# Other starting steps for the background work of a three-layer kernel on one TensorE

## The chip, the cores and the metric

The kernel runs on one core of a Trainium2 chip. The metric is the device time of one execution in microseconds (us); less is better. Inputs and output lie in the chip's memory; the weights arrive as 64-bit floats, everything else as 32-bit floats.

## The reference, cut to what matters

```python
def _attn_ref(q, k, v):                      # q, k, v: (8, 8, 576, 64)
    q_s = exp(q - max(q, -1));  q_s /= sum(q_s, -1) + 1e-9
    k_s = exp(k - max(k, 2));   k_s /= sum(k_s, 2) + 1e-9
    return q_s @ (k_s^T @ v)                 # per batch and head
x = attn.transpose(0, 2, 1, 3).reshape(4608, 512)
h = x @ w_in                                 # (512, 2048)
x = max(0.01 * h, h) @ w_out                 # (2048, 512)     layer A
h = max(max(x @ w1, x @ w2), x @ w3)         # (512, 768) each
out = h @ w_out2                             # (768, 512)      layer B
```

## The kernel before, in words

The 4608 tokens are nine chunks of 512. Every matrix product is done in three matmuls of 32-bit halves (high by high, high by low, low by high), 128 by 128 by 512, so an operand first has to be split into a high and a low part: ScalarE (ACT) copies the high part, VectorE (DVE) subtracts it.

**Foreground.** The foreground is counted in steps. Steps 0 to 47 are layer A for chunks 0 to 2, one step for one of the 16 blocks of 128 hidden columns (24 matmuls: `project` and `a_out`). Steps 48 to 79, 80 to 111 and 112 to 143 are layer A for the chunk pairs (3, 4), (5, 6), (7, 8), by a seven-product scheme. In each pair a left half has eight rounds `t` of three steps; a round has seven products of six matmuls (`product_a`, L798, weights in tiles `group`) and four fills of six (`out_a`, L570, weights in tiles `outw`). The right half has 16 blocks `m` of 12 matmuls, two to a step, and reads a new `outw` tile of 1 MB every step. Then come layer B for chunk 0 (six blocks `m`, L1172) and, to the end, layer B for four pairs, which has no background beside it.

**Background.** `background(step)` is called once in a step, and twice from step 28 to 47. It starts the generators whose time has come (`plan_units`, `ahead_units`) and moves each running one to its next `yield`. They are: attention of later chunks (`kv_unit`, `q_unit`: two loads, reductions, exponentials, small matmuls, for each chunk and pair of heads); `sums_a`, the weight sums of layer A (eight, each two loads, four additions, a split, stores to `stream_in`); `ahead_unit` u = 0 to 8, layer B's first weights (two loads, each converted from 64 bits by `split_words`; sums; two splits; stores to `stream` and `plainw`); `ahead_out` m = 0 to 5, layer B's second weights (one load, one conversion, one store `wo`); and `join`, which adds the partial results of chunks 0 and 1.

**What sets the order.** A planner puts the instructions on each engine in the order in which its own timeline has them ready, the earlier written first. Background work on DVE is tied to its step by a one-column copy from the newest `g` (L165, L322). The loads of `group` and `outw` are pinned: each is issued behind the last DMA written before it. All DMAs are issued by one queue, SP's, in order; an issue that waits holds up every one behind it. `group` and `outw` are loaded two tiles ahead.

**Buffers that matter.** `wp` has 17 tiles of 8 KB a partition, shared by weights, operands and rooms. `xp` has two tiles each of `xhi` and `xlo`; rooms of `ahead_unit` and `ahead_out` alternate between the two. `ca` is a single buffer: each conversion and each high part (`hi`) of an `ahead_unit` takes it in turn, and a `hi` keeps it until its stores have landed.

Of the kernel before, what the change touches and what calls it, by code (L numbers as in the profile page):

```python
# [18 lines left out]
P = 128  # L19
# [7 lines left out]
CONV = 3  # L27
HALVES = 28
APAIRS = ((3, 4), (5, 6), (7, 8))
AUSES = ("a11", "a12", "s2", "s1", "s3", "a22", "s4")  # L30
# [39 lines left out]
def tile_kernel(ctx: ExitStack, tc: tile.TileContext, q, k, v, wa, wb, out):  # L70
# [72 lines left out]
    def post():  # L143

        for f in posted[:]:
            f()
        posted.clear()

    def split_words(raw, hi, lo, n, after=None, whole=None, keep=None):

        if raw.dtype != I64:
            if whole is not None:
                nc.vector.tensor_copy(whole, raw.rearrange("p (b n) -> p b n", n=H))
                return
            if keep is not None:
                posted.append(lambda: nc.sync.dma_start(keep, raw[:, :N]))
            nc.scalar.activation(hi, raw, AF.Copy)
            nc.vector.tensor_tensor(lo, raw, hi.bitcast(F32), op=ALU.subtract)
            return
        words = raw.bitcast(U32).rearrange("p (n t) -> p n t", t=2)  # L160
        high, low = words[:, :, 1], words[:, :, 0]
        a = cp.tile([P, 2 * N], U32, tag="ca", name="ca")[:, :n]
        af, bf = a.bitcast(F32), high.bitcast(F32)
        if after is not None:
            nc.scalar.activation(af[:, 0:1], after[:, 0:1], AF.Copy)  # L165
        nc.scalar.activation(af, bf, AF.Abs)
        nc.vector.tensor_scalar(af, af, MOST_HIGH, LEAST_HIGH, op0=ALU.min, op1=ALU.max)
        nc.vector.tensor_scalar(a, a, 3, 0x3FFFFFF8, op0=ALU.logical_shift_left, op1=ALU.bitwise_and)
        nc.vector.scalar_tensor_tensor(a, high, 0xC0000000, a, op0=ALU.bitwise_and, op1=ALU.bitwise_or)
        if whole is None:  # L170
            nc.scalar.activation(hi, af, AF.Copy)
        nc.vector.tensor_scalar(high, a, 0xFF800000, None, op0=ALU.bitwise_and)
        nc.vector.scalar_tensor_tensor(bf, low, 2.0**-52, bf, op0=ALU.mult, op1=ALU.mult)
        if whole is not None:
            af, bf = (t.rearrange("p (b n) -> p b n", n=H) for t in (af, bf))
            nc.vector.tensor_tensor(whole, af, bf, op=ALU.add)
            return
        nc.vector.tensor_tensor(af, af, bf, op=ALU.add)
        nc.vector.tensor_tensor(lo, af, hi.bitcast(F32), op=ALU.subtract)
        if keep is not None:  # L180
            copy = raw.bitcast(F32)[:, :N]
            nc.scalar.activation(copy, af[:, :N], AF.Copy)
            posted.append(lambda: nc.sync.dma_start(keep, copy))

# [54 lines left out]

    def a_room():  # L240
        rooms.append(xp.tile([P, 4 * N], F32, tag=("xhi", "xlo")[len(rooms) % 2], name="room"))
        return rooms[-1]

    def ahead_unit(u):

        t, j = UNITS[u]
        room = a_room()
        b = room.rearrange("p (b n) -> p b n", n=H)
# [24 lines left out]
    def ahead_out(m):  # L273
        room = a_room()
        raw = room[:, 2 * N :].bitcast(wb.dtype)[:, :N]
# [40 lines left out]
    def behind_step(column):  # L316
# [4 lines left out]
        if "g" in newest:  # L321
            nc.scalar.activation(column, newest["g"][:, 0:1], AF.Copy)  # L322

    def hurried(c):
        return CONV <= c < CONV + 2

# [8 lines left out]
    def kv_unit(b, hp, early):  # L335
# [46 lines left out]
        else:  # L382
# [7 lines left out]
            nc.scalar.activation(ke, ke, AF.Exp)  # L390
            if hurried(b):
                yield
        yield
# [49 lines left out]
    def q_unit(c, hp, early):  # L443
# [69 lines left out]
        yield  # L513
        if hurried(c):
            yield
        while not kv_done(c, hp):
# [120 lines left out]
    def sums_a(t):  # L637

        room = wp.tile([P, 4 * N], F32, tag="w", name="room")
        b = room.rearrange("p (b n) -> p b n", n=H)  # L640
# [21 lines left out]
    def plan_units(c):  # L662

        early = c < EARLY
        for hp in range(NP):
            if c == 2:
                start, lag = 2 * hp + 13, 2
            elif c < CONV + 2:
                start, lag = HALVES + (c - CONV) * 6 + 1.5 * hp, 1
            else:  # L670
                i, at = divmod(c - CONV, 2)
                start, lag = CONV * MA + 2 * MA * (i - 1) - 8 + 3 * (4 * at + hp), 2
            if c < B:
                yield start, kv_unit(c, hp, early)
            if c == EARLY:
                yield HALVES, split_kv_unit(c - 1, hp)
            yield start + lag, q_unit(c, hp, early)
# [23 lines left out]
    def ahead_units():  # L701
        for m in range(MA):
            yield max(BEGUN[m] + 3, 8), stage_a(m)
        for t in range(MA // 2):
            yield HALVES + 2 + 2.5 * t, sums_a(t)
        for u, at in enumerate((52, 64, 84, 100, 112, 116, 124, 128, 132)):
            yield at, ahead_unit(u)
        for m, at in enumerate((90, 94, 119, 122, 135, 137)):
            yield at, ahead_out(m)
        for c, at in enumerate((112, 123)):  # L710
            yield at, join(c)
# [121 lines left out]
    for turn in turns:  # L833
# [3 lines left out]
        for m in range(*turn[1:]):  # L837
# [14 lines left out]
            if step == 0:  # L852
# [7 lines left out]
                conv_a(2, x_tiles(1)[0][:, NP - 1].bitcast(F32))  # L860
            if step >= HALVES:
                background(step + 0.5)
            step += 1
            if step > CONV * MA - 4:
                if not begun_a:
                    building = a_operands(0, begun_a)
                    begun_a["begun"] = True
                for _ in range(3 if step < CONV * MA else 99):
                    next(building, None)
            if step == CONV * MA - 2:  # L870
                for i in range(AHEAD_A + 1):
# [17 lines left out]
    def store_pair(i, side, f, acc):  # L889
# [7 lines left out]

        posted.append(rows)

# [25 lines left out]
    for i in range(len(APAIRS)):  # L925
# [47 lines left out]
        for m in range(MA - 2):  # L973
# [10 lines left out]
            if last and m == 11:  # L984
                cur = split_x2(loaded)
            if m == 2 and not last:
                building = a_operands(i + 1, nxt)
            if 2 <= m:
                for _ in range(1 if m < MA - 3 else 99):
# [5 lines left out]
        fills = [lambda f=f, i=i, pairs=pairs: out_a(i, 1, MA // 2 - 1, f, pairs) for f in range(KDM)]  # L995
    assert not live and not waiting
    att_ctx.close()
    bp.append(ctx.enter_context(tc.tile_pool(name="bp", bufs=1)))

    def store_rows(i, c, col, acc):  # L1000
# [171 lines left out]
    for m in range(MB):  # L1172
        if m < 4:
            for i in range(4 + 2 * m, 6 + 2 * m):
                load_b(i)
        accs3 = [project_b(m, j, cur) for j in range(3)]
        g = f32_tile()
# [9 lines left out]
        else:  # L1187
            b_out(*prev)
        if m == 1:
            ops = {}  # L1190
            building = operands(quarters_b(sides), ops, operand)
        if m >= 2:
            for _ in range(2 if m < MB - 1 else 99):
                next(building, None)
        if m == 3:
            for i in range(AHEAD):
                load_group(i)
        prev = (0, m, hpair)
# [92 lines left out]
```

## Time and profile before

| | |
|---|---|
| median of three runs | 1484.92 us (1484.3 to 1485.85) |
| profiled execution | 1488.23 us, its span 1486.4 us |
| TensorE busy | 1405.0 us, 95% |
| VectorE, ScalarE busy | 886.2 us (60%), 679.7 us (46%) |
| moved by DMA | 343.99 MB, 231 GB/s over the span |
| steps 24 to 47 | about 177 to 351 us |
| pair 0, left and right half | about 351 to 496 and 496 to 558 us |
| pair 1, left and right half | about 558 to 676 and 676 to 728 us |
| pair 2, left and right half | about 728 to 868 and 868 to 938 us |
| layer B of chunk 0 | about 938 to 1000 us |

The stages are cut where the count of matmuls of each line says that a step begins; the planner lets a round's first product slip before the end of the stage ahead of it, so the edges are not sharp. The granted clock (PEclk) is the share of TensorE's full 2.4 GHz in a stretch; its other level is 1.2 GHz. A busy TensorE at a low clock does less.

### The profile page before, as it was taken

The page shows a single profiled execution, that of the slowest core. Times are in us where ns is not written, and L with a number is a line of the kernel's source. Part 1 is how long each engine was busy: PE and PEld are TensorE (multiplying, and loading weights), DVE is VectorE, ACT ScalarE, POOL GpSimd, SP SyncE. Part 2 cuts the span into 40 slices and gives each one's busy share as a digit, 9 for nine tenths or more (in the row PEclk, how much of TensorE's full clock was granted, in tenths as well). Part 3 has the DMA queues.
Part 4 walks back from the last instruction along what each step waited for, and adds up shares of the span by engine and source line. Part 5 has one row for each costly group of instructions (what it writes and reads, how often), then busy time and mean ns, then how long its engine had stood idle before and what let it go on. Part 6 is the DMA issues. An engine that isn't in the chain of part 4 may idle for free.

```text
span 1486.4 us, 18291 instructions
## 1 busy us (share of the span) xinstructions
PE 1405.0 (95%) x6624; PEld 1138.1 (77%) x6624; DVE 886.2 (60%) x1468; ACT 679.7 (46%) x1400; POOL 25.3 (2%) x42
## 2 busy tenths in 40 slices
PE   7999999998999899999997766999999999999999
PEld 5788877786888678887775655888888888888887
DVE  9888958987676836748556564323562463454332
ACT  6766846665565636645343332312242233233222
POOL 0000001000000000000000000000000000000000
PEclk9999999999999999999998988999999999999999
DMA  9487957555866855777988887947334724634701
GB/s 375 163 285 250 319 194 225 159 195 178 338 245 252 286 230 217 273 285 284 372 301 314 299 294 238 408 175 282 142 114 135 286 89 184 241 142 140 280 13 57
DMA packets 127194, 343.99 MB, mean 231 GB/s; under 512 B 11392, under 2 KB 68224, under 8 KB 102656
## 3 DMA queue, kind: packets, MB, share of 16 engines
q1 hardware_dynamic: 127104, 342.83, 63.4%
q8 instruction: 52, 0.85, 0.2%
q14 instruction: 38, 0.31, 0.1%
HBM read 257.33 MB, written 85.46 MB: 231 GB/s over the span
## 4 chain that ended last, share of the span: by engine, by line
PE 79%; DMA 8%; DVE 7%; ACT 3%; issue 2%; SPq 1%; DVEq 0%; ACTq 0%
PE ps L798 36%; PE acc L570 31%; PE ps L570 10%; DMA outw<-stream_out 1%; PE ps L398 1%; DMA room<-wi 1%; PE ps L522 1%; DMA spare<-in_v_dram 1%; DMA stream<-hi 1%; DMA spare<-in_k_dram 1%; DVE opA L759 1%; DVE glo L591 1%; DMA stream_out<-w 1%; DMA raw<-in_wa_dram 1%; DMA room<-in_wb_dram 1%
## 5 line engine op out<-in xcount | busy, mean ns | idle before, releaser
L798 PE MATMUL ps<-op,group 128*128 128x512 f32 x1512 | 352.8, 389 | 0.7 <-ACT snap L1090 0.7
L798 PEld LDWEIGHTS ps<-op,group 128*128 128x128 f32 x1512 | 283.6, 188 | 60.2 <-ACT snap L1090 1.3
L570 PE MATMUL acc<-ghi,outw 128*128 128x512 f32 x768 | 255.2, 400 | 36.0 <-DMA outw<-stream_out 33.9
L798 PE MATMUL ps<-opA,group 128*128 128x512 f32 x1008 | 252.4, 396 | 11.7 <-DMA group<-stream_in 7.8
L798 PEld LDWEIGHTS ps<-opA,group 128*128 128x128 f32 x1008 | 189.2, 190 | 56.0 <-DMA group<-stream_in 8.2
L570 PEld LDWEIGHTS acc<-ghi,outw 128*128 128x128 f32 x768 | 147.2, 193 | 71.0 <-issue 35.0
L570 PE MATMUL acc<-glo,outw 128*128 128x512 f32 x384 | 154.0, 401 | 4.4 <-DVE glo L591 4.4
L570 PE MATMUL acc<-wB,h 128*128 128x512 f32 x576 | 140.4, 389 | 0.1
L570 PE MATMUL acc<-ghi,w 128*128 128x512 f32 x384 | 128.3, 397 | 3.6 <-ACT ghi L590 3.6
L570 PE MATMUL ps<-xhi,w 128*128 128x512 f32 x384 | 128.9, 401 | 1.3 <-ACT g L845 0.7
L1090 ACT ACTIVATE snap<-ps 128x512 f32<-128x512 f32 x108 | 61.8, 598 | 143.8 <-PE ps L798 143.2
L570 PEld LDWEIGHTS acc<-wB,h 128*128 128x128 f32 x576 | 108.0, 188 | 23.3 <-ACT h L1114 0.5
L1105 DVE TENSOR_TENSOR snap<-snap,ps 128x512 f32<-128x512 f32 x72 | 49.4, 686 | 119.0 <-ACT snap L1090 92.4
L591 DVE TENSOR_TENSOR glo<-g,ghi 128x512 fp32r<-128x512 f32 x102 | 69.8, 687 | 46.6 <-ACT ghi L590 46.1
L570 PEld LDWEIGHTS acc<-glo,outw 128*128 128x128 f32 x384 | 74.1, 193 | 23.1 <-DVE glo L591 7.7
L570 PEld LDWEIGHTS ps<-xhi,w 128*128 128x128 f32 x384 | 73.5, 192 | 18.3 <-ACT g L845 1.1
L570 PEld LDWEIGHTS acc<-ghi,w 128*128 128x128 f32 x384 | 72.1, 189 | 20.0 <-ACT ghi L590 4.7
L1101 DVE TENSOR_TENSOR best<-snap,ps 128x512 f32<-128x512 f32 x36 | 24.7, 687 | 93.7 <-PE ps L798 43.8
L590 ACT ACTIVATE ghi<-g 128x512 fp32r<-128x512 f32 x102 | 63.6, 628 | 29.1 <-PE acc L570 13.8
L570 PE MATMUL acc<-glo,w 128*128 128x512 f32 x192 | 75.6, 394 | 1.0 <-DVE glo L591 1.0
L570 PE MATMUL ps<-xlo,w 128*128 128x512 f32 x192 | 76.2, 398 | 0.1
L1114 ACT ACTIVATE h<-best 128x512 fp32r<-128x512 f32 x48 | 30.3, 632 | 95.6 <-DVE best L1107 95.2
(159 smaller groups left out, 1799.7 us busy)
## 6 DMA issues: line engine op xcount, KB each, us to landing
group<-stream SPq DMA_DIRECT2D x64, 1024.0 KB, 6.6
outw<-stream_out SPq DMA_DIRECT2D x48, 1024.0 KB, 8.8
group<-stream_in SPq DMA_DIRECT2D x42, 1024.0 KB, 8.9
raw<-in_wa_dram SPq DMA_DIRECT2D x16, 1024.0 KB, 7.6
room<-in_wb_dram SPq DMA_DIRECT2D x24, 512.0 KB, 5.4
x<-st SPq DMA_DIRECT2D x40, 256.0 KB, 2.9
wB<-plainw SPq DMA_DIRECT2D x9, 1024.0 KB, 14.3
stream_out<-w SPq DMA_DIRECT2D x16, 512.0 KB, 4.2
```

The costliest lines, as they stand in the source:

```text
L398: nc.tensor.matmul(acc[z, : D + 1], lhsT=ke[:, r, z], rhs=vt[:, r, h], start=r == 0, stop=r == RK - 1)
L522: nc.tensor.matmul(both(xps, c0, c1), lhsT=a, rhs=halves(y, c0, c1), start=i == 0, stop=i == 2)
L570: nc.tensor.matmul(acc, lhsT=l, rhs=r, start=first and i == 0, stop=last and i == 2)
L590: nc.scalar.activation(hi[:, z], g[:, z], AF.Copy)
L591: nc.vector.tensor_tensor(lo[:, z], g[:, z], hi[:, z].bitcast(F32), op=ALU.subtract)
L759: nc.vector.tensor_tensor(o[:, 1, z], t[:, z], o[:, 0, z].bitcast(F32), op=ALU.subtract)
L798: nc.tensor.matmul(bank, lhsT=l, rhs=r, start=fresh and first, stop=last, skip_group_check=not fresh)
L1090: nc.scalar.activation(t, bank, AF.Copy)
L1101: nc.vector.tensor_tensor(g, snap, bank, op=ALU.add)
L1105: nc.vector.tensor_tensor(snap, snap, bank, op=ALU.add)
L1114: nc.scalar.activation(h[:, m, 0], g, AF.Copy)
```

## The change

It changes no arithmetic of the result. Attention of chunks 3 and 4 starts at the steps of `HURRIED`, three to four steps earlier, and later chunks' five steps later and closer together; a yield is added in both generators. Four of the eight `sums_a` move from steps 30 to 47 into pair 0. The nine `ahead_unit`s and six `ahead_out`s get other steps: none is left in pair 0, five pieces lie in pair 1, and the last two begin in layer B's first blocks, where `background` is now called nine times more. The last three units and two outs take their rooms from `wp`. Operands of the next pair are built from block 5 of the right half, not 2; those of pair 0 over five steps. The store of the first weights' copy (`keep`) is written two background calls later. Layer B's own pool, operands and weights 8 to 11 come at its block 3.

```diff
+HURRIED = ((24, 2), (26, 2), (28, 1), (29.5, 1), (31, 1), (32.5, 1), (34, 1), (35.5, 1))
     def post():
-        for f in posted[:]:
+        now = [f for wait, f in posted if wait == 0]
+        posted[:] = [(wait - 1, f) for wait, f in posted if wait]
+        for f in now:
             f()
-        posted.clear()
...
-            posted.append(lambda: nc.sync.dma_start(keep, copy))
+            posted.append((2, lambda: nc.sync.dma_start(keep, copy)))
...
-    def a_room():
+    def a_room(wide=False):
+        if wide:
+            return wp.tile([P, 4 * N], F32, tag="w", name="room")
...
-        room = a_room()                       # ahead_unit
+        room = a_room(t == 2)
...
-        room = a_room()                       # ahead_out
+        room = a_room(m >= 4)
...
-            if hurried(b):                    # kv_unit, behind the exponential
-                yield
+            yield
...
-        if hurried(c):                        # q_unit, ahead of its matmuls
-            yield
+        yield
...
-        room = wp.tile([P, 4 * N], F32, tag="w", name="room")    # sums_a
+        room = a_room(t < 4)
...
             elif c < CONV + 2:
-                start, lag = HALVES + (c - CONV) * 6 + 1.5 * hp, 1
+                start, lag = HURRIED[4 * (c - CONV) + hp]
             else:
                 i, at = divmod(c - CONV, 2)
-                start, lag = CONV * MA + 2 * MA * (i - 1) - 8 + 3 * (4 * at + hp), 2
+                start, lag = CONV * MA + 2 * MA * (i - 1) - 3 + 2.5 * (4 * at + hp), 2
...
-                yield HALVES, split_kv_unit(c - 1, hp)
+                yield 27, split_kv_unit(c - 1, hp)
...
-            yield HALVES + 2 + 2.5 * t, sums_a(t)
-        for u, at in enumerate((52, 64, 84, 100, 112, 116, 124, 128, 132)):
+            yield (30, 34, 38, 42, 49, 53, 57, 61)[t], sums_a(t)
+        for u, at in enumerate((88, 93, 98, 112, 117, 122, 133, 137, 141)):
             yield at, ahead_unit(u)
-        for m, at in enumerate((90, 94, 119, 122, 135, 137)):
+        for m, at in enumerate((103, 107, 127, 131, 144, 147)):
             yield at, ahead_out(m)
-        for c, at in enumerate((112, 123)):
+        for c, at in enumerate((112, 124)):
             yield at, join(c)
...
-            if step >= HALVES:
-                background(step + 0.5)
-            step += 1
-            if step > CONV * MA - 4:
+            building_a = step >= CONV * MA - 5
+            if building_a:
                 if not begun_a:
                     building = a_operands(0, begun_a)
                     begun_a["begun"] = True
-                for _ in range(3 if step < CONV * MA else 99):
+                next(building, None)
+            if step >= HALVES:
+                background(step + 0.5)
+            if building_a:
+                for _ in range(1 if step < CONV * MA - 1 else 99):
                     next(building, None)
+            step += 1
...
-            if m == 2 and not last:
+            if m == 5 and not last:
                 building = a_operands(i + 1, nxt)
-            if 2 <= m:
+            if 5 <= m:
...
     load_b(3)
     for m in range(MB):
-        if m < 4:
-            for i in range(4 + 2 * m, 6 + 2 * m):
-                load_b(i)
-        accs3 = [project_b(m, j, cur) for j in range(3)]
+        for i in {0: (4, 5), 1: (6, 7), 3: (8, 9, 10, 11)}.get(m, ()):
+            load_b(i)
+        if m == 3:
+            assert not live and not waiting and not posted
+            att_ctx.close()
+            bp.append(ctx.enter_context(tc.tile_pool(name="bp", bufs=1)))
+            ops = {}
+            building = operands(quarters_b(sides), ops, operand)
+            for i in range(AHEAD):
+                load_group(i)
+        accs3 = []
+        for j in range(3):
+            accs3.append(project_b(m, j, cur))
+            if m < 3:
+                background(step)
+                step += 1
...
-        if m >= 2:
-            for _ in range(2 if m < MB - 1 else 99):
+        if m >= 3:
+            for _ in range(3 if m < MB - 1 else 99):
                 next(building, None)
```

## Rows read from the trace of the kernel before

**Rows 1.** The page's first part: busy us, share of the span, instructions.

```profile
PE 1405.0 (95%) x6624; PEld 1138.1 (77%) x6624; DVE 886.2 (60%) x1468; ACT 679.7 (46%) x1400; POOL 25.3 (2%) x42
```

**Rows 2.** Stretches by stage: length, busy (instructions) by engine, clock, DMA share, GB/s.

```profile
177.00:351.00 174.00, 161.64 (x879) 129.15 (x879) 133.25 (x244) 105.00 (x257) 8.34 (x10) 0.96 0.60 199
...
558.00:676.00 118.00, 116.27 (x532) 95.53 (x531) 75.23 (x139) 66.96 (x154) 0.70 (x1) 1.00 0.69 250
676.00:728.00 52.00, 52.00 (x231) 43.05 (x230) 33.99 (x42) 23.00 (x35) 0.00 (x0) 1.00 0.95 358
728.00:868.00 140.00, 120.80 (x494) 95.01 (x493) 80.46 (x127) 57.67 (x101) 0.00 (x0) 0.93 0.83 310
868.00:938.00 70.00, 44.46 (x175) 35.54 (x175) 32.80 (x53) 21.21 (x36) 0.00 (x0) 0.80 0.78 275
938.00:1000.00 62.00, 62.00 (x275) 51.34 (x275) 23.00 (x37) 15.59 (x27) 0.00 (x0) 1.00 0.74 288
```

**Rows 3.** Stretches of 20 us, the same columns.

```profile
320.00:340.00 20.00, 14.87 (x66) 11.98 (x64) 20.00 (x27) 11.98 (x22) 0.70 (x1) 0.99 0.72 279
...
480.00:500.00 20.00, 17.27 (x78) 11.76 (x77) 18.95 (x33) 15.81 (x31) 0.04 (x1) 0.91 0.65 240
...
700.00:720.00 20.00, 20.00 (x90) 16.57 (x89) 8.44 (x14) 5.13 (x9) 0.00 (x0) 1.00 1.01 406
...
800.00:820.00 20.00, 12.15 (x42) 9.19 (x42) 13.92 (x20) 5.71 (x11) 0.00 (x0) 0.74 0.92 354
820.00:840.00 20.00, 20.00 (x90) 16.53 (x89) 12.56 (x20) 8.54 (x14) 0.00 (x0) 1.00 0.96 364
840.00:860.00 20.00, 11.68 (x40) 9.11 (x39) 6.82 (x12) 5.41 (x10) 0.00 (x0) 0.74 0.70 244
...
880.00:900.00 20.00, 9.34 (x30) 7.52 (x31) 11.74 (x21) 4.77 (x9) 0.00 (x0) 0.66 0.82 294
...
920.00:940.00 20.00, 10.50 (x38) 8.52 (x39) 3.30 (x6) 1.42 (x3) 0.00 (x0) 0.66 0.87 332
```

**Rows 4.** Waits from 790 to 950 us: total, times, longest, in us.

```profile
PE acc L570 <- DMA outw<-stream_out: 33.9, 3, 14.3
...
ACT ca L165 <- DMA stream<-hi: 16.3, 4, 10.5
...
PE ps L798 <- DMA group<-stream_in: 7.8, 1, 7.8
```

**Rows 5.** SP's waits from 790 to 950 us, the same columns.

```profile
SPq L282 <- DVE room L179: 21.1, 3, 11.2
```

**Rows 6.** SP's issues in order of time: start, length in us, line, tiles.

```profile
922.01 0.32 SPq L282 DMA_DIRECT2D wo<-room  x1
922.42 0.38 SPq L821 DMA_DIRECT2D outw<-stream_out  x1
```

**Rows 7.** VectorE by line and shape: total us, mean ns, idle before.

```profile
L385 DVE TENSOR_REDUCE mx<-ke 128x128 f32<-128x640 f32 x24 | 31.3, 1304 | 0.4 <-ACT mx L322 0.4
...
L487 DVE TENSOR_TENSOR qt<-qt,qsm 128x512 f32<-128x512 f32 x28 | 19.3, 690 | 0.6
...
L235 DVE TENSOR_TENSOR room<-room,hi 128x1024 fp32r<-128x1024 f32 x8 | 9.9, 1242 | 1.9 <-ACT hi L234 1.9
L226 DVE TENSOR_TENSOR room<-room 128x256 f32<-128x256 f32 x17 | 7.2, 421 | 11.1 <-DMA room<-wi 10.8
```

**Rows 8.** DMA issues by tile: count, KB each, median us to landing.

```profile
outw<-stream_out SPq DMA_DIRECT2D x48, 1024.0 KB, 8.8
...
room<-in_wb_dram SPq DMA_DIRECT2D x24, 512.0 KB, 5.4
...
stream<-hi SPq DMA_DIRECT2D x19, 256.0 KB, 4.8
...
plainw<-hi SPq DMA_DIRECT2D x9, 512.0 KB, 8.7
...
stream<-hi SPq DMA_DIRECT2D x28, 128.0 KB, 3.9
```

More of the change, by code (lines that the diff above doesn't have):

```diff
@@ L155, in split_words @@
             if keep is not None:
-                posted.append(lambda: nc.sync.dma_start(keep, raw[:, :N]))
+                posted.append((0, lambda: nc.sync.dma_start(keep, raw[:, :N])))
             nc.scalar.activation(hi, raw, AF.Copy)
@@ L322, in behind_step @@
             nc.scalar.activation(column, newest["g"][:, 0:1], AF.Copy)
-    def hurried(c):
-        return CONV <= c < CONV + 2
     multiplied = set()
@@ L896, in rows @@
                 nc.sync.dma_start(x2[c, 0, MA][:, f, side * H : side * H + H], st[:, at * H : at * H + H])
-        posted.append(rows)
+        posted.append((0, rows))
     def out_a(i, side, t, f, pairs, ms=(0, 1)):
@@ L995, in tile_kernel @@
         fills = [lambda f=f, i=i, pairs=pairs: out_a(i, 1, MA // 2 - 1, f, pairs) for f in range(KDM)]
-    assert not live and not waiting
-    att_ctx.close()
-    bp.append(ctx.enter_context(tc.tile_pool(name="bp", bufs=1)))
     def store_rows(i, c, col, acc):
@@ L1188, in tile_kernel @@
             b_out(*prev)
-        if m == 1:
-            ops = {}
-            building = operands(quarters_b(sides), ops, operand)
-        if m >= 2:
-            for _ in range(2 if m < MB - 1 else 99):
+        if m >= 3:
+            for _ in range(3 if m < MB - 1 else 99):
                 next(building, None)
-        if m == 3:
-            for i in range(AHEAD):
-                load_group(i)
         prev = (0, m, hpair)
```

## The prediction

> **What bounds the kernel now.** I read the page's first part, then the stretches by stage, then the waits of the worst stretch, then SP's queue in it. TensorE is busy 1405 us [rows 1], so nearly everything is a question of where it stands still or runs at a low clock. An undisturbed 20 us holds 90 matmuls (820 to 840) [rows 3], 0.222 us each; I use that to turn missing matmuls into time.
>
> The reader is to see three places. From 938 us on there is almost nothing to win: 62.0 busy of 62, and no background behind it [rows 2]. Pair 2 is the worst: four stretches of 20 us hold 42, 40, 30 and 38 matmuls instead of 90 [rows 3], 210 missing, 46.7 us. By stage, 494 and 175 matmuls are worth 148.6 us and took 210 [rows 2]; the difference of 61 us is the upper bound, since some records can be missing. I take 47 to 61 us as lost there. Steps 24 to 47 are the second: 174 us for 161.6 us of busy time at a mean clock of 0.96 [rows 2], so 12.4 us idle and about 0.04 x 174 = 7 us of slow clock, 19 us. There VectorE is the neighbour that is late: 20.00 busy of 20 while TensorE has 14.87, from 320 to 340 us [rows 3]. The third is small: 2.7 us idle and 0.09 x 20 = 1.8 us of clock where pair 0's halves meet, again beside a VectorE at 18.95, from 480 to 500 us [rows 3].
>
> What ends the waits in pair 2: TensorE stands 33.9 us in three waits for an `outw` tile and 7.8 us for a `group` [rows 4]. Those loads wait in SP's queue: `wo<-room` of an `ahead_out` goes out at 922.01 and the pinned `outw` load right behind it at 922.42 [rows 6], after SP had waited up to 11.2 us for the conversion that the store needs [rows 5]. That conversion was late since `ca` was taken: ScalarE waited for `ca` until stores of a `hi` had landed, 16.3 us in four waits, the longest 10.5 [rows 4]. So a chain of four (store of `hi`, `ca`, conversion, blocked queue) ends in TensorE. It is not the amount of DMA: pair 2 runs at 310 and 275 GB/s [rows 2], while 406 GB/s were moved from 700 to 720 us with TensorE full [rows 3].
>
> **Steps 24 to 47.** Four `sums_a` leave, each one subtraction of 1.24 us and four additions of 0.42 [rows 7], 2.9 us, together 11.7. Of chunk 5, three `kv` units started at 40, 43 and 46 and two `q` units at 42 and 45; now the first start is 45. A `kv` unit has its reduction at 1.30 and a subtraction I take as half to two thirds of that; a `q` unit has six passes of about 0.69 [rows 7], 4.1. I take 11 us as leaving. VectorE falls from 133 to some 110 us, against TensorE's 161.6 x 0.96 = 155: from 86% to 71%. The attention of chunks 3 and 4, begun up to four steps earlier, keeps its amount but is spread wider; operands, spread over five steps, are late one step less. I take 12 of the 19 us, least 4, most 19. What is late next is ScalarE, 105 of 174 [rows 2]. The copy's store, two calls later, holds a tile of a full `wp` two steps longer when the last weights come; as it isn't pinned it may go out when its data is ready, so I price it at 0, at worst 6 us, one step.
>
> **Pair 0.** `ahead_unit` 0 and 1 go, four `sums_a` come, and building starts three blocks later, clear of attention's tail. Of the 4.5 us, gain 3 (0 to 5). Loads and stores of a sums unit are few and small; SP passes them quickly.
>
> **Pair 1** gets unit 0 to 2 and outs 0 and 1: five pieces for four. VectorE has room, 75 of 118 us [rows 2]. But the pieces now stand closer, and I count collisions on `ca`. A unit converts at its 2nd and 4th step, and takes `ca` for `hi` at the 6th and 7th, freed by stores written a step later. With a distance of 5, unit 1's conversion at 95 meets unit 0's second `hi` at 95; unit 2's does so at 100; out 0's at 105, in the right half, where each step eats an `outw`. The last is the relation of unit 8 (132) and out 5 (137) before, which ended in the 14.3 us wait [rows 4]. The DMA beside it is lighter than layer B's weights made it there, but 358 GB/s were already moved in that half [rows 2]. I charge 5 us (0 to 20).
>
> **Pair 2** moves nearly as much as before. A unit loads 2 x 512 KB, stores 2 x 512 to `plainw` and 2 x (19 x 256 + 28 x 128) / 9 = 1877 KB to `stream` [rows 8]: 3.9 MB. Before, units 4 to 8 and four outs; now units 3 to 7, some of 8 and two outs: the 310 GB/s x 140 + 275 x 70 = 62.7 MB [rows 2] stay within 2 MB. What changes is the collisions. Before, conversions met a held `ca` at 118, 124, 130, 134 and 139, and the right half also had outs at 135 and 137, whose stores stand ahead of a pinned load; after, at 119, 124, 129 and 139, and no out is left in the right half. Rooms of units 6 to 8 come from `wp`, so they no longer wait for joins and for `xhi`, `xlo`. Of the right half's six `outw` loads, I find one behind a store or load that must wait for `ca` (unit 7's second load, at 139), against three before. A stall cost 46.7 / 4 = 11.7 us; I leave one and a half, 17 us, of 47: gain 30. The least is 8 (three remain), the most 47.
>
> The Trainium skill, "DMA: Bandwidth & Descriptors", section "Bandwidth", has a limit against this change: some 358 GB/s for a core between the chip's memory and SBUF. By it the same 62.7 MB would need 175 us, so pair 2 could win 35 of its 210 at most; the 406 GB/s stretch [rows 3] says that it isn't a hard limit here, and TensorE's own 149 us then bounds it. My 30 holds under both.
>
> **Layer B's start.** Units 7 and 8 end and outs 4 and 5 run there: two conversions and two stores, a unit's stores and half of another's, some 6 to 7 MB (from the 3.9 MB above). They come into 62 us that moved 288 GB/s [rows 2], 17.9 MB; 25 MB in 62 us is 400 GB/s, just under the best stretch. Weights 8 to 11 move back a block and the pair's operands two, so the peak is lower at first. Behind a late weight tile stand its 12 matmuls and all later ones. Price 3 us (0 to 12). The operands have three blocks, 31 us, for VectorE work that was done in four beside 23.0 of 62 us busy; hidden.
>
> **Sum.** -12 - 3 + 5 - 30 + 3 = -37 us. Against the profiled execution's 1488.2 that is 1451; that execution lies 3.3 us over the median, so 1484.9 - 37 = 1448 us.
>
> **Rivals.**
> - *The chain only moves.* Units stay four and five steps apart, nine steps long, with one `ca`; every conversion still meets a `hi`. Then pair 2 gives 10, pair 1 costs 10, layer B 6, the early steps give 10 and pair 0 gives 2: -6, 1479 us. For it: the count of collisions hardly falls. Against: in pair 2's left half the same collisions at 118 and 130 cost nothing, as 820 to 840 shows 90 matmuls [rows 3].
> - *All of it goes.* Pair 2 loses only 5 us, the early steps 3: -42 - 16 - 3, 1424 us. For it: the prefetch of two tiles covers a shorter wait. Against: 62.7 MB in 155 us is 404 GB/s, the best stretch all along.
> - *Slower: layer B waits for the tail.* Its pool opens only when every unit has ended, at block 3. Units 6 to 8 and two outs need `ca` for about 3 x 4 + 2 = 14 turns from step 133; at the longest wait of 10.5 us [rows 4] a turn, 147 us, while the foreground needs 15 + 43 + 31 = 89 us to block 3. A stall of up to 58 us, less the slack of 20 us that the last operands have, is +38; with pair 2's right half still losing its 25 and the three collisions of pair 1 at 11.7 each, +35, and gains of 15 in the early steps and 22 in pair 2's left half: +36, about 1521; it turns slower than before from some 8 us a turn. Against: four waits averaged 4.1 us [rows 4].
> - *Nothing moves*, since the planner places what isn't tied to a step where it was: 1484 us. Against: conversions are tied through L165.
>
> **How the numbers follow.** Forecast 0.55, chain moves 0.15, all goes 0.18, slower 0.08, nothing 0.04. A measurement of this kernel tells 0.2%, 3 us, from no change. Faster by more: 0.55 + 0.18 + 0.15 = 0.88; within: 0.04; slower: 0.08. The likeliest's own range is the sum's ends taken half way, 1430 to 1466; both unknowns of pair 1 and pair 2 at their ends give 1414 to 1479, and with the first two rivals I say 1416 to 1480.
>
> **What would show it.** Right: no stretch of 20 us with VectorE full near 320 us; waits for `outw` in pair 2 down from 33.9 to 10 to 17 us; clock of pair 2's stages at 0.95 or over; a wait of 3 to 10 us for `outw` in pair 1's right half; layer B's first blocks without a gap over 3 us. Wrong: `outw` waits of over 25 us, or a wait at block 3 for `op`. The prediction as a whole is wrong if pair 2 keeps its 210 us, or if pair 1's right half grows by more than 15.

## The result, and the profile after

The changed kernel takes 1501.27 us (median of four runs, 1500.22 to 1502.32), beside 1485.38 us for the kernel before on the same chip: a ratio of 1.0108, 95% interval 1.0091 to 1.0126. It is slower by 1.1%; 1448 us were forecast, with 1416 to 1480 as the range. Its profiled execution has a span of 1500.2 us, 13.8 more than before.

The sums of work did not move. The first part of the page after, to be laid beside [rows 1]:

```profile
PE 1404.6 (94%) x6624; PEld 1139.9 (76%) x6624; DVE 887.9 (59%) x1468; ACT 681.2 (45%) x1400; POOL 26.1 (2%) x42
```

So the whole story is where TensorE stands. Stretches of the kernel after, cut at the same steps as [rows 2]: steps 24 to 47, pair 1's right half, pair 2's left and right half, layer B of chunk 0 (columns: from and to, length, busy time and instructions of TensorE, weight load, VectorE, ScalarE and GpSimd, clock, DMA share, GB/s):

```profile
177.00:342.00 165.00, 158.76 (x864) 127.58 (x864) 124.05 (x220) 102.58 (x244) 7.42 (x9) 0.99 0.57 191
664.00:725.00 61.00, 56.21 (x225) 45.00 (x226) 38.23 (x53) 23.48 (x35) 0.00 (x0) 0.93 0.88 330
725.00:882.00 157.00, 120.75 (x497) 96.66 (x496) 79.40 (x122) 57.61 (x102) 0.00 (x0) 0.89 0.76 279
882.00:925.00 43.00, 40.95 (x173) 33.40 (x174) 21.20 (x35) 15.63 (x28) 0.00 (x0) 0.96 0.85 309
925.00:1014.00 89.00, 66.89 (x277) 54.10 (x276) 48.80 (x81) 25.14 (x42) 0.00 (x0) 0.87 0.83 311
```

Length against length with [rows 2], the five stages went 174 to 165 (-9), 52 to 61 (+9), 140 to 157 (+17), 70 to 43 (-27) and 62 to 89 (+27). The right half of pair 1 begins at 664 instead of 676, so steps 48 to 103 gave another 3. The sum is -12 + 9 + 17 - 27 + 27 = +14, the difference of the spans. The edges are not sharp: the counts of matmuls in a stage differ by up to 15 from [rows 2], some 3 us. What left pair 2's right half came back, in length, in layer B. The last column is a mean over a stage and hides much: 279 and 311 GB/s are made of stretches in which the DMA engines were full and of others in which they had little to do.

Four stretches of 20 us of the kernel after, the same columns:

```profile
320.00:340.00 20.00, 20.00 (x90) 16.57 (x89) 9.35 (x15) 7.52 (x12) 0.70 (x1) 1.00 0.49 168
480.00:500.00 20.00, 20.00 (x90) 16.55 (x89) 14.86 (x16) 12.45 (x23) 1.60 (x1) 1.00 0.90 338
800.00:820.00 20.00, 2.01 (x9) 1.31 (x7) 11.36 (x16) 4.53 (x7) 0.00 (x0) 0.65 0.81 279
980.00:1000.00 20.00, 3.03 (x12) 2.17 (x12) 10.00 (x17) 5.17 (x8) 0.00 (x0) 0.67 0.62 206
```

The first two answer to [rows 3]: VectorE falls from 20.00 and 18.95 busy to 9.35 and 14.86, and TensorE is full in both. The last two are the new holes: 9 and 12 matmuls where 90 fit. Three stretches that come before a hole, the same columns:

```profile
760.00:780.00 20.00, 20.00 (x90) 16.58 (x89) 7.83 (x13) 9.12 (x17) 0.00 (x0) 1.00 1.02 408
790.00:800.00 10.00, 10.00 (x45) 8.29 (x45) 7.91 (x14) 4.02 (x7) 0.00 (x0) 1.00 0.19 55
920.00:960.00 40.00, 37.78 (x161) 30.87 (x160) 20.63 (x35) 11.94 (x20) 0.00 (x0) 0.96 1.03 393
```

So ahead of each hole the DMA engines were full for 20 to 40 us (share 1.02 and 1.03). The waits of the kernel after, 640 to 1060 us (total, times, longest), name what TensorE stood for:

```profile
PE ps L797 <- DMA group<-stream_in: 23.7, 2, 19.1
...
ACT ca L167 <- DMA stream<-hi: 20.7, 6, 7.1
PE ps L569 <- DMA wB<-plainw: 19.9, 2, 19.3
...
PE acc L569 <- DMA outw<-stream_out: 19.3, 5, 9.3
```

Against [rows 4], the waits for `outw` fell from 33.9 to 19.3 us, but a `group` rose from 7.8 to 23.7 and a tile `wB` of layer B's first weights came new with 19.9.

**The hole at 801 us.** SP's issues in order of time in the kernel after (start, length, line, tiles), cut to the five that matter:

```profile
769.95 0.33 SPq L255 DMA_DIRECT2D room<-in_wb_dram  x1
772.01 0.32 SPq L688 DMA_DIRECT2D xf<-x  x1
797.21 0.32 SPq L691 DMA_DIRECT2D part<-x  x1
804.62 1.29 SPq L221 DMA_DIRECT2D stream<-hi  x3
...
815.11 1.34 SPq L808 DMA_DIRECT2D group<-stream_in  x2
```

SP issued nothing for 25 us in front of a join's `part`, then nothing for 7 us in front of the stores of a unit; the `group` that TensorE wanted from 801.6 us on stands behind both. The unit is unit 4, begun at step 117: its stores to `plainw` are the fifth pair of the nine. (The expectations of e2, e7 and e11 call it unit 5.) ScalarE of the same kernel, from the touch of `ca` for that unit's second conversion (L167) to that conversion (L168):

```profile
769.95 0.20 ACT L167 ACTIVATE ca<-g 128x1 f32<-128x1 f32 x1
...
791.17 0.60 ACT L919 ACTIVATE g<-ps 128x512 f32<-128x512 f32 x1 [4.80 <-PE ps L797]
791.66 0.65 ACT L168 ACTIVATE ca<-room 128x512 f32<-128x512 f32 x1
```

The conversion came 21.7 us after its touch, and the larger part of that was a load. The `room` of line 255 that SP issued at 769.95, which the conversion reads, took this long to land (the view of L255 from 769 to 771 us):

```profile
DMA to landing us min/median/max: 16.9/16.9/16.9
```

It landed at 786.9 us, since it was issued into the full stretch of 760 to 780 us. Only the last 4.8 us are ScalarE's order: the conversion stood behind a foreground copy (`g<-ps`) that waited for TensorE. What frees the tile for `part` is VectorE's addition of the `part` before it, and that stands in VectorE's order behind the conversion's first steps; it ends at 797.18, just before the issue at 797.21:

```profile
794.83 2.35 DVE L696 TENSOR_TENSOR xf<-xf,part 128x1024 f32<-128x1024 f32 x2
```

The sums and stores of the unit came after it. Meanwhile the DMA engines ran dry (55 GB/s from 790 to 800 us), as SP issued nothing.

**The hole at 983 us.** SP's issues of the kernel after around it:

```profile
975.62 0.32 SPq L295 DMA_DIRECT2D wB<-plainw  x1
985.53 0.32 SPq L286 DMA_DIRECT2D wo<-room  x1
986.58 1.31 SPq L221 DMA_DIRECT2D stream<-hi  x3
...
993.96 0.52 SPq L273 DMA_DIRECT2D plainw<-room  x1
...
997.26 0.32 SPq L295 DMA_DIRECT2D wB<-plainw  x1
```

The `wB` at 997.26 is the copy of unit 8's weights, which unit 8 itself stored at 993.96. Unit 8 begins at step 141 now, not 132, and is the last of a row of units and outs that take `ca` by turns. The row was held up by the full DMA: ScalarE had unit 7's first `hi` ready at 931.8 us, and it held `ca` until its stores had landed, at 958.8 us. SP issued those stores only at 945.78 us, behind layer B's weights and operands, and they took 10.1 to 12.1 us to land in the full stretch of 920 to 960 us. TensorE stood from 983.4 to 1002.8.

### The profile page after: what moved, and what is told of

It is laid out like the page before. It is cut to its first block, busy times and chain, and to the rows that moved or that the text cites. A ratio compares the mean times of both kernels' runs of the same rounds, so it can differ in the third digit from the quotient of the medians.

```text
span 1500.2 us, 18253 instructions
## 1 busy us (share of the span) xinstructions
PE 1404.6 (94%) x6624; PEld 1139.9 (76%) x6624; DVE 887.9 (59%) x1468; ACT 681.2 (45%) x1400; POOL 26.1 (2%) x42
## 4 chain that ended last, share of the span: by engine, by line
PE 81%; DMA 8%; DVE 5%; ACT 3%; SPq 1%; issue 1%; ACTq 0%; DVEq 0%
PE ps L797 36%; PE acc L569 32%; PE ps L569 11%; DMA outw<-stream_out 2%; DMA wB<-plainw 2%; PE ps L398 1%; PE ps L521 1%; DMA stream<-hi 1%; DMA group<-stream_in 1%; DMA stream_out<-w 1%; SPq L221 1%; ACT hi L265 1%; DMA plainw<-room 0%; PE ps L493 0%; DVE ca L171 0%
## 5 line engine op out<-in xcount | busy, mean ns | idle before, releaser
L797 PE MATMUL ps<-opA,group 128*128 128x512 f32 x1008 | 253.9, 398 | 29.5 <-DMA group<-stream_in 23.7
L569 PE MATMUL acc<-ghi,outw 128*128 128x512 f32 x768 | 256.4, 400 | 22.6 <-DMA outw<-stream_out 19.3
L589 ACT ACTIVATE ghi<-g 128x512 fp32r<-128x512 f32 x102 | 63.7, 630 | 36.0 <-DVE g L1190 22.8
```

The lines of the kernel that those rows point to most:

```text
L569: nc.tensor.matmul(acc, lhsT=l, rhs=r, start=first and i == 0, stop=last and i == 2)
L589: nc.scalar.activation(hi[:, z], g[:, z], AF.Copy)
L797: nc.tensor.matmul(bank, lhsT=l, rhs=r, start=fresh and first, stop=last, skip_group_check=not fresh)
```

## The experiments

Two theories stood at first. *Chain*: the late placing makes the units and outs, which share one `ca`, end too late, and every loss behind step 104 is that chain's. *Shape*: single new neighbours are to blame, the joins beside unit 4 in one place, the order of the last weights in the other. All times are ratios to the kernel before, measured on the same chip, with a 95% interval.

**e1_early: the late part undone.** Steps of units, outs and joins, their rooms, and layer B's start as before; the attention, `sums_a`, operand and `keep` edits stay.

```diff
-        for u, at in enumerate((88, 93, 98, 112, 117, 122, 133, 137, 141)):
+        for u, at in enumerate((52, 64, 84, 100, 112, 116, 124, 128, 132)):
...
-        for m, at in enumerate((103, 107, 127, 131, 144, 147)):
+        for m, at in enumerate((90, 94, 119, 122, 135, 137)):
```

> The changed kernel with the late part undone: units, outs and joins at their steps of before, all rooms from xp, layer B's start as before; the moves of attention, of the sums, of the operands and of the copy's store are kept. Theory (the early part gained what was forecast, the late part lost it): the changed kernel reached step 48 about 14 us earlier and lost 8 us less where pair 0's halves meet, so this runs about 18 us under before, 1467 us (ratio 0.988). Rival (the early gain needs units 0 and 1 out of pair 0, or is given back in pair 2 all the same): within 5 us of before, 1480 to 1490.

Measured 1473.89 us, 0.9904 (0.9883 to 0.9926), between the theory's time and the rival's. The early part is worth about 14 us and the late part costs 1.0108 - 0.9904 = 0.0204, 30 us. Its waits from 560 to 1060 us are those of before [rows 4]:

```profile
PE acc L569 <- DMA outw<-stream_out: 33.7, 3, 15.4
...
ACT ca L167 <- DMA stream<-hi: 22.6, 6, 10.5
...
PE ps L797 <- DMA group<-stream_in: 8.6, 1, 8.6
```

**e2_joins: both joins out of pair 2.**

```diff
-        for c, at in enumerate((112, 124)):
+        for c, at in enumerate((66, 77)):
```

> The changed kernel with both joins begun in pair 0, at steps 66 and 77, instead of in pair 2. Theory (the 19 us wait for a group at 801 comes from the second join: its part load has one xlo tile, VectorE's additions wait for that load, and unit 5's sums and the queue stand behind them): that wait falls under 4 us, and pair 2 loses 9 MB; 1501 - 20 to 25 = 1476 to 1481, less if pair 0 pays. Rival (collisions on ca make that wait, joins are only beside it): the wait stays over 10 us, time 1495 or more.

Measured 1469.61 us, 0.9884 (0.9864 to 0.9903): 33 us less than the change and more of a gain than the theory had. The hole at 801 us is gone, and unit 4's second conversion now follows its touch by 8 us, as ScalarE's rows of this kernel show; the `wB` wait stays.

```profile
767.58 0.19 ACT L167 ACTIVATE ca<-g 128x1 f32<-128x1 f32 x1
...
775.57 0.67 ACT L168 ACTIVATE ca<-room 128x512 f32<-128x512 f32 x1
```

The load that it reads was issued at 765.45 and took 9.0 us to land, not 16.9 (L255 from 765 to 766 us):

```profile
DMA to landing us min/median/max: 9.0/9.0/9.0
```

**e3_cb: conversions out of `ca`.** Conversions of 512 columns use the two halves of `plain` by turns, so `ca` is left to the `hi` parts.

```diff
+        if n > N:
+            a = cp.tile([P, 2 * N], U32, tag="ca", name="ca")
+        else:
+            turned.append(n)
+            at = len(turned) % 2 * N
+            a = plain.rearrange("p a b -> p (a b)").bitcast(U32)[:, at : at + N]
-        a = cp.tile([P, 2 * N], U32, tag="ca", name="ca")[:, :n]
```

> The changed kernel with the conversions of 512 columns (units and outs) taken from ca to two halves of the tile plain, which is unused by then; ca is left to the high parts alone. Theory (a conversion waits for ca until a high part's stores have landed): ScalarE's waits for ca on DMA stream<-hi vanish, outw waits fall from 19 us to under 8, the wait at layer B's block 4 halves: 1501 - 25 to 35 = 1466 to 1476. Rival (the join and the plain order on the queue set the waits): 1490 to 1500, with the waits for group and wB as long as before.

Measured 1446.03 us, 0.9722 (0.9707 to 0.9737): with the steps of the change untouched, 1.0108 - 0.9722 = 0.0386, 57 us, some 20 more than the theory had. The DMA is as full as in the change (416 GB/s from 760 to 780 us), so a full DMA alone does not make a hole of 19 us. Its waits from 560 to 1060 us; no row of `ca` behind a store is left, and in pair 1's right half no wait of over 1.4 us:

```profile
PE ps L576 <- DMA wB<-plainw: 11.6, 2, 7.8
...
PE ps L804 <- DMA group<-stream_in: 8.2, 1, 8.2
...
PE acc L576 <- DMA outw<-stream_out: 1.2, 1, 1.2
```

**e4_wb: the last weights from early copies.**

```diff
-            nc.sync.dma_start(w.bitcast(F32), plainw[u])
+            nc.sync.dma_start(w.bitcast(F32), plainw[u % 6])
```

> The changed kernel, but layer B's weights of its last two blocks are loaded for chunk 0 from the copies of units 3 to 5, not 6 to 8 (other numbers enter the products of chunk 0). Theory (the 20 us wait in layer B's block 4 is for unit 8, begun at 141 and stored only at 994 us): no wait for wB over 3 us, 1501 - 20 to 24 = 1477 to 1481. Rival (layer B's pool and operands wait for the tail anyway): the wait moves to op or group at block 3 to 6 and the time stays at 1495 or more.

Measured 1495.34 us, 1.0055 (1.0036 to 1.0074). Some 8 us come of the 20 that the wait had, so the rival's time came. The wait is gone, and the waits of this kernel show what was late next, a `wB` that comes from an out and a `group` whose `stream` the units store:

```profile
PE acc L569 <- DMA wB<-wo: 5.4, 1, 5.4
...
PE ps L797 <- DMA group<-stream: 4.8, 1, 4.8
```

Not one tile but the end of the whole row of units and outs is late.

**e5_before_cb: the same edit as e3 in the kernel before.**

```diff
-        a = cp.tile([P, 2 * N], U32, tag="ca", name="ca")[:, :n]
...
+            a = plain.rearrange("p a b -> p (a b)").bitcast(U32)[:, at : at + N]
```

> The kernel before with the one edit of e3_cb: conversions of 512 columns take two halves of plain, ca is left to the high parts. Theory (the collisions on ca made two of the three outw waits of before, 26 of 33.9 us, and the slow clock behind them; the 8 us wait for a group is the join's): 1485 - 30 to 40 = 1445 to 1455, waits for outw under 8 us. Rival (ca is only the place where full DMA queues show): less than 15 us gained, 1470 or more.

Measured 1449.04 us, 0.9752 (0.9727 to 0.9776): the shared `ca` cost the kernel before 36 us. Its `outw` waits, 33.9 us in [rows 4], are now:

```profile
PE ps L805 <- DMA group<-stream_in: 5.5, 1, 5.5
...
PE acc L577 <- DMA outw<-stream_out: 4.7, 1, 4.7
```

**e6_early_cb: e1 and e3 together.**

```diff
-        for u, at in enumerate((88, 93, 98, 112, 117, 122, 133, 137, 141)):
+        for u, at in enumerate((52, 64, 84, 100, 112, 116, 124, 128, 132)):
...
+            a = plain.rearrange("p a b -> p (a b)").bitcast(U32)[:, at : at + N]
```

> Both at once: the early part alone (e1_early, 14 us under before) and conversions outside ca. Theory (they act in different stages and add): e5_before_cb less 14, about 1436 us, and under e3_cb's 1446, so that the late part costs even where ca is no bound. Rival (with ca gone the late part is harmless or a gain): 1446 or more.

Measured 1442.26 us, 0.9704 (0.9677 to 0.973). Beside e3's 0.9722, whose interval it overlaps, the late part now costs 0.0018, some 3 us that the intervals don't tell from none, where it cost 30 with `ca` shared. So neither the theory nor the rival is shown. The early part is worth 0.9752 - 0.9704, 7 us, there.

**e7_partw: a join's `part` from `wp`.** In the hole at 801 us SP stood first before a `part` whose tile the `part` before it held until VectorE had added it. If that tile is the cause, another pool ends it.

```diff
-            part = xp.tile([P, KDM, N], F32, tag="xlo", name="part")
+            part = wp.tile([P, KDM, N], F32, tag="w", name="part")
```

> The changed kernel with the joins' part tiles in the pool wp instead of xp's xlo, joins at their steps. Theory (the queue stood from 772 to 797 us since a part had to wait for its only xlo tile, that is for VectorE's additions of the part before): the 19 us wait for a group goes under 5, about 1480 to 1486 us. Rival (the additions' place in VectorE's order holds up unit 5 whatever the tile): wait over 10 us, 1493 or more.

Measured 1499.49 us, 1.0093 (1.0062 to 1.0124), no change that can be told. That theory fell. SP now stands in the same place before unit 4's stores; SP's issues of this kernel:

```profile
772.41 0.33 SPq L255 DMA_DIRECT2D room<-in_wb_dram  x1
802.09 1.30 SPq L221 DMA_DIRECT2D stream<-hi  x3
```

Whatever stands first in the queue waits for the same late conversion (at 794.33 here; its load took 14.4 us to land).

**e8_best1: conversions out of `ca`, joins in pair 0, units every five steps and outs in the gaps, nothing begun in layer B, all rooms from `xp`.**

```diff
-        room = a_room(t == 2)
+        room = a_room()
...
-        room = a_room(m >= 4)
+        room = a_room()
...
+        for u, at in enumerate((88, 93, 98, 106, 112, 117, 122, 127, 132)):
+        for m, at in enumerate((110, 114, 119, 124, 129, 134)):
+        for c, at in enumerate((66, 77)):
```

> The changed kernel with conversions outside ca, joins at 66 and 77, units at 88, 93, 98, 106, 112, 117, 122, 127, 132 and outs at 110, 114, 119, 124, 129, 134, all rooms in xp, so that nothing is left for layer B. Theory (ca, the joins beside the units and the late last units are what the late part lost): e3_cb's 8 us wait for a group and its 12 us of waits for wB go, 1446 - 20 to 25 = 1421 to 1426. Rival (pair 2 is bound by the amount moved): its stretch still holds over 15 us of waits and the time is 1440 or more.

Measured 1425.07 us, 0.9592 (0.9566 to 0.9618). It beats both kernels by 60 and 76 us. Stretches of this kernel, the columns as above: from 640 to 920 us, about steps 104 to 143, and the best 20 us.

```profile
640.00:920.00 280.00, 269.83 (x1165) 218.41 (x1164) 178.37 (x291) 127.98 (x223) 0.00 (x0) 0.99 0.97 357
680.00:700.00 20.00, 20.00 (x90) 16.57 (x89) 15.56 (x24) 9.50 (x15) 0.00 (x0) 1.00 1.03 409
```

**e9_cb_joins: e3 with the joins of e2.**

```diff
+            a = plain.rearrange("p a b -> p (a b)").bitcast(U32)[:, at : at + N]
...
+        for c, at in enumerate((66, 77)):
```

> The changed kernel with conversions outside ca and joins at 66 and 77, units and outs as in the change. Theory (three separate losses): the 8 us group wait of e3_cb goes, the waits for wB of the late last units stay, 1446 - 8 to 10 = 1436 to 1438. Rival (the joins' gain in e2_joins was through ca): within 3 us of e3_cb, 1443 or more.

Measured 1431.3 us, 0.9624 (0.9608 to 0.9641). The joins are worth another 0.0098, 15 us, on top of e3, more than the theory had, and less than the 33 us without it: so more than half of e2's gain came of the joins and the shared `ca` together. Its waits from 560 to 1060 us have one row left for TensorE of over 2 us, at layer B's start, where the steps of the change still end late (e8, whose units end earlier, has no wait for a `wB`):

```profile
PE ps L576 <- DMA wB<-plainw: 12.6, 2, 7.5
```

**e10_best1_ca: e8 with the conversions back in `ca`.** The reverse of e3's edit.

```diff
-            a = plain.rearrange("p a b -> p (a b)").bitcast(U32)[:, at : at + N]
+        a = cp.tile([P, 2 * N], U32, tag="ca", name="ca")[:, :n]
```

> e8_best1 with the conversions back in ca. Theory (ca turns a denser pair 2 into waits, whatever the steps): waits for outw and group over 20 us again, 1425 + 25 to 40 = 1450 to 1465. Rival (the new steps and joins do it, ca is not needed): under 1435.

Measured 1510.21 us, 1.0149 (1.0129 to 1.0169). The best kernel becomes the slowest of all: 0.0557 of the time, 83 us, by this one buffer, more than was expected. Its waits from 560 to 1060 us:

```profile
PE acc L569 <- ACT ghi L589: 34.0, 7, 12.4
...
PE acc L569 <- DMA outw<-stream_out: 26.3, 4, 10.6
...
ACT hi L265 <- DMA stream<-hi: 24.6, 7, 11.0
ACT ca L167 <- DMA stream<-hi: 23.4, 7, 5.9
...
PE ps L797 <- DMA group<-stream_in: 15.9, 1, 15.9
```

ScalarE waits 48 us for stores, as against 1.2 in e8. The largest wait of TensorE is for no load at all: while ScalarE stands in front of `ca`, the foreground's next split (`ghi`, L589) stands behind it in ScalarE's order. In e10 ScalarE waits 5.94 us for stores before it touches `ca` at 782.64 us, splits at 784.06, and TensorE, which had stood for 12.4 us, goes on at 784.74. So a shared `ca` costs in two ways, SP's queue and ScalarE's order. The three placements in which it was measured (e5, e3, e10) cost 36, 57 and 83 us; they differ in the joins and rooms too, so that closeness of the units alone raises the price is not shown.

**e11_join132: only the second join moved, eight steps later.**

```diff
-        for c, at in enumerate((112, 124)):
+        for c, at in enumerate((112, 132)):
```

> The changed kernel with its second join begun at 132 instead of 124, so that the same bytes move in pair 2 but not beside unit 5. Theory (the place beside unit 5's second conversion makes the 19 us wait, not the bytes): that wait falls under 6 us, 1501 - 15 to 22 = 1479 to 1486, if the right half does not pay for the join. Rival (the bytes of the join): the wait only moves, over 10 us in pair 2's end, 1495 or more.

Measured 1488.0 us, 1.0007 (0.9996 to 1.0018), between the theory's time and the rival's. A wait of 19.6 us stays in the same place, now for an `outw`, so the second join beside that unit is not needed for it. The 15 us that it gains on the change come from elsewhere. The waits from 560 to 1060 us:

```profile
PE acc L569 <- DMA outw<-stream_out: 37.4, 6, 19.6
...
PE ps L569 <- DMA wB<-plainw: 19.3, 1, 19.3
```

Of the runs with the units' steps of the change, only taking both joins out (e2) or the conversions out of `ca` (e3, e9) shortens that hole. Of the joins, their bytes are part of it: the load of unit 4's second conversion took 16.9 us to land in the change, 14.4 in e7, 13.4 here and 9.0 in e2, and the conversion came 4.8, 7.5, 2.9 and 1.2 us after that. How much each of the bytes, VectorE's additions and ScalarE's order is worth stays open.

## Why the prediction was wrong

**Steps 24 to 47 and pair 0: right.** Forecast -12 and -3, measured -9 and, over steps 48 to 103, -3 in the stretches, and -14 together in e1. VectorE fell to 124 us, not to 110, but had 9.35 of 20 us at 320, where it had been full, and TensorE no longer waits there.

**Pair 1's right half: the sign right, the path in part another.** Forecast +5 (0 to 20), measured +9. An `outw` behind an out's store was named, and one stands there (issued behind `wo` at 691 us), but it cost 0.4 us. In the stage TensorE is idle for 4.8 us, of which 4.4 are a wait for an operand of the next pair (`opA`, L757) that stood behind an out's touch of `ca` in ScalarE's order; the slow clock (0.93 over 61 us) makes some 4 more. An `outw` wait of 5.4 us ends just ahead of the stage, behind a unit's load. When conversions leave `ca` (e3), no wait of over 1.4 us is left there.

**Pair 2: the step that failed.** The forecast was -30 for the whole pair; it was +17 on the left and -27 on the right, together 210 to 200, -10. The right half was read rightly: with no out left in it, 2 us stand still (43 less 40.95). In the left half I had counted that conversions still meet a held `ca` at 119, 124 and 129, and yet left "one and a half, 17 us," of stalls for the whole pair: the count of blocked loads took only the right half's six `outw` loads, and the loads of the left half got no term. The left half alone now has 36 us without a matmul, 157 less 120.75. What let me leave so little was the sentence that "the same collisions at 118 and 130 cost nothing": one undisturbed stretch of before [rows 3], taken as a rule. It showed only that the two prefetched tiles had been enough there. A collision has no price of its own; it costs what its wait exceeds the slack of what stands behind it, a pinned load in SP's queue or a foreground copy on ScalarE. After, one conversion came 21.7 us behind its touch, 16.9 of them a load on full DMA engines, and the cover of two tiles was gone. That the last units' rooms no longer come from `xp`, which I counted as relief, was not tried alone; e8 has every room in `xp` and is the fastest.

**Layer B's start: the term that was mis-sized most.** Forecast +3 (0 to 12), measured +27. I priced it by bytes, "25 MB in 62 us is 400 GB/s". The bytes came (311 GB/s over 89 us are 27.7 MB; at the 406 GB/s of [rows 3] that is 68 us), and what I left out is what they do to `ca`: in the full stretch of 920 to 960 us one `hi` held it for 27 us. TensorE was then busy still, and stood later, with 206 GB/s moving, when bytes were no longer the limit. What ended last was a row of turns: the last units and outs take `ca` one after another, and unit 8's copy is ready when the row ends. I had this as the slower rival, with a chance of 0.08, for a wait at block 3 of up to 58 us, less slack; it came as a wait of 19.3 us for the last unit's own weights. Of its total of 1521 the runs give 1501. e4 shows that it is the end of the row and not one tile.

**The rival "the chain only moves"** had for it that "the count of collisions hardly falls". That was the sentence to believe. Its terms came nearly all: the early steps gave 9 (10 forecast), pair 1's right half cost 9 (10), pair 2 gave 10 (10), steps 48 to 103 gave 3 (pair 0, 2). Only layer B, put at 6, cost 27, and so its total of 1479 us was missed as well.

**The range was narrower than its terms.** "1414 to 1479" does not come out of pair 1 and pair 2 at their ends, which give 1426 to 1485. With all five terms at their best ends the sum gives 1414, at their worst -4 + 0 + 20 - 8 + 12 = +20, 1505 us, and the measured 1501 lies inside that. That the pair would move as many bytes within 2 MB was off too: 279 GB/s x 157 us and 309 x 43 are 57 MB, not 62.7.

**What the sum left out.** The price of the shared `ca` could be bounded before: I knew the chain from the store of a `hi` to TensorE, and took it as a number of single stalls of 11.7 us each. e5, e3 and e10 measure the buffer itself: 36 us in the kernel before, 57 with the change, 83 with the steps of e8. Once that price is gone, this late part is worth next to nothing either way (e6 beside e3), while other steps are worth 0.9722 - 0.9592 = 0.0130, 19 us (e8 beside e3, of which the joins are 15 by e9).

**The amount of DMA** was taken as no limit, from means over stages. That holds for the means, but in full stretches (408 GB/s from 760 to 780 us, 393 from 920 to 960) loads and stores landed late, and the shared `ca` handed that on. The same bytes without the shared `ca` (e3) make waits of 8 us, not of 19. The Trainium skill, "DMA: Bandwidth & Descriptors", section "Bandwidth", gives about 358 GB/s as what each core gets when both cores of a pair stream. This kernel runs on one core, and e8 moved 357 over 280 us on average, at a DMA share of 0.97, and 409 from 680 to 700 us, so 358 is no ceiling here and the prediction's use of it as a limit did not bear on this kernel. The DMA may be what bounds the background of e8 next; no run tested that.

## What to carry to other kernels

Before background work is moved, list the single buffers it passes through and how long each is held; a buffer that is freed only when a store has landed serialises everything that takes it, and holds up what stands behind it on the engine that waits for it. Give that buffer a second copy first (here two halves of a tile that lay idle), and choose the steps afterwards. And in a queue that issues in order, price a late store by the loads that stand behind it and by how far ahead those were issued. A stage's mean GB/s does not tell whether loads land late; stretches of 10 to 40 us do.

## What the runs showed that was not expected

A background instruction's delay need not show as a wait of its own: 21.7 us passed between touch and conversion with no idle time charged to the conversion. For 16.9 of them its load was in flight, but ScalarE's idle time in it is charged to TensorE, for which the foreground copies in front of the conversion waited. Only the time from issue to landing tells the two apart.

While TensorE stands, its clock falls as well: the two 20-us stretches with 9 and 12 matmuls show 0.65 and 0.67, a mean of its two levels (0.50, the lower one, from 810 to 820 us, where there is no matmul), and the change's four stages from step 104 on lie at 0.87 to 0.96, beside 0.99 over the 280 us of e8. For the same 6624 matmuls TensorE is busy 1389.6 us in e8's profile (below) and 1404.6 in the change's: 15 us that I read as what the slow clock behind the stalls costs beyond their own length.

```profile
PE 1389.6 (98%) x6624; PEld 1130.1 (79%) x6624; DVE 883.2 (62%) x1468; ACT 677.2 (48%) x1400; POOL 25.0 (2%) x42
```

This is the first part of e8's page. VectorE and ScalarE, with the same instructions, are within 5 us of the change.
